# A mixture-of-experts layer's first product as seven block products instead of eight

## The chip, the core and the metric

The kernel runs on one core of one Trainium2 chip. The metric is the device time of one execution in microseconds; the median of three runs before the change is 1262.46 us. The profile is of one further execution. Engines carry their short names in the rows: PE is TensorE's matmuls, PEld its weight loads, DVE is VectorE, ACT ScalarE, POOL GpSimd, SP the engine that issues the transfers.

## The reference, cut to what matters

Three layers stand one behind the other: an attention over 32 packed queries, a dense layer pair (MoE1, 512 to 2048 to 512), and MoE2, four experts whose outputs are added with weights per token. All tensors are float32; there are 2304 tokens.

```python
def _moe_ref(x, w_in, w_out):                 # MoE1
    h = x @ w_in                              # 2304x512 @ 512x2048
    g = h * (1.0 / (1.0 + np.exp(-1.702 * h)))
    return (g @ w_out).astype(np.float32)

def _moe2_ref(x, domain_probs, w1, w2):       # MoE2
    E = w1.shape[0]                           # 4 experts, w1: 4x512x1024, w2: 4x1024x512
    p = domain_probs / (domain_probs.sum(-1, keepdims=True) + 1e-09)
    out = np.zeros((N, D), dtype=np.float32)
    for e in range(E):
        h = np.maximum(x @ w1[e], 0.0)        # first product
        out += p[:, e:e + 1] * (h @ w2[e])    # second product
    return out.astype(np.float32)
```

## The kernel before, in words

Every large product is computed in three parts: each operand is split into a high half (a cast, by ScalarE) and a low half (the operand less the high half, by VectorE or GpSimd), and three matmuls add high times high, low times high and high times low into one PSUM bank (`PARTS`). The helper `split` (L155 to L157) does both steps.

Up to some 240 us the attention runs, mixed with the first conversions and the begin of MoE1; its order is written out by a planner (`Order`) inside a manually scheduled block. Behind that block stands the rest of MoE1 and all of MoE2 as a list of steps `moe`, issued in the order of the list; the framework orders each engine's instructions from that and from what is ready.

MoE1 makes four passes `a` over its 2048 features, each over eight blocks `j` of 288 tokens. `l1_first` (matmuls on L523) makes the hidden features, `l2_first` (L568) sums 12 matmuls into a bank, and `l2_out` adds the bank to the accumulator `ACC[j]` (ScalarE copies in the first pass on L588, VectorE adds later on L590). In the last pass `put_y` splits each result into high and low halves, with GpSimd making the low half; this is `Y`, the moving operand of MoE2.

MoE2 takes the 32 chunks of 128 hidden features (4 experts x 8) in eight passes of four chunks. In each pass it walks five token blocks of 512, 512, 512, 256 and 512 tokens. `l1_second` streams the block's 512 or 256 tokens against 12 weight tiles (4 slices of the 512 inputs x 3 parts, L607); ScalarE takes the relu as the high half (L616) and VectorE makes the low half from the same bank (L617). One step later `l2_second` multiplies each 128 tokens of it by the 512 columns of w2 (L632), summing all four chunks of the pass in one bank per 128 tokens; then one VectorE instruction scales by the token's probability and adds to the output accumulator `ACC2` (L651; ScalarE in the first pass, L649). Each chunk's weights are loaded once (two transfers of 256 KB, L192 and L196) and split by ScalarE and VectorE. In the last pass SP sends out each 128 tokens (L655).

All large tiles come from one pool, `big`, with 37 buffers and the single tag `b`, through `slot`. PSUM is one pool of eight banks, `psum`. The conversion of MoE1's weights (`convert`) uses a small pool of its own, `cv`.

Of the kernel before, what the change touches and what calls it, by code (L numbers as in the profile page):

```python
# [97 lines left out]
def packed_attention_moe_kernel(  # L98
# [446 lines left out]
    def put_y(t, tok, n, src):  # L545

        done = 0
        while done < n:
# [12 lines left out]

    def l2_first(a, j, t):
# [21 lines left out]
    def l2_out(a, j, t, ps):
        dst = ACC[j][:, t, :]
        yield ("ACT" if a == 0 else "DVE"), 0.45, 0
        if a == 0:
            nc.scalar.copy(out=dst, in_=ps[:, :HS])  # L588
        else:
            nc.vector.tensor_add(out=dst, in0=ps[:, :HS], in1=dst)  # L590
# [1 line left out]
        if a == n_pass1 - 1:
            put_y(t, j * HS, HS, dst)


    n_pass2 = len(chunks2) // CPP
    per_e = w1.shape[2] // 128 // CPP
# [2 lines left out]
    def l1_second(a, j, c):  # L600
        n = blocks[j][1]
        w = W["x", a * CPP + c, 0]
        ps = psum("ps_g")
        m = 0
        for wp, xp in PARTS:
            for kk in range(KD):
                nc.tensor.matmul(  # L607
                    out=ps[:, :n],
                    lhsT=w[:, wp, kk * 128:(kk + 1) * 128],
                    rhs=Y[j, kk][:, xp, :],  # L610
                    start=(m == 0),
                    stop=(m == 3 * KD - 1),
                )
# [7 lines left out]
        hid[a, j, c, 2] = h

    def l2_second(a, j, c):
        b0, n = blocks[j]
        w = W["x", a * CPP + c, 1]
        h = hid.pop((a, j, c, 2))
        nt = n // 128
        if c == 0:
            accs[j] = [psum("ps_o") for _ in range(nt)]
        for t in range(nt):  # L630
            for m, (wp, hq) in enumerate(PARTS):
                nc.tensor.matmul(  # L632
                    out=accs[j][t],
                    lhsT=h[:, hq, t * 128:(t + 1) * 128],
                    rhs=w[:, wp, :],
                    start=(c == 0 and m == 0),
                    stop=(c == CPP - 1 and m == 2),
                )
# [209 lines left out]
```

## Time and profile before

| | |
|---|---|
| three runs, us | 1261.56, 1262.46, 1264.24 |
| profiled execution, us | 1263.64 |
| its span from first to last instruction, us | 1261.5 |
| TensorE busy / mean granted clock | 1205.0 us (96%) / 0.973 |
| VectorE, ScalarE, GpSimd busy | 538.9, 380.8, 116.4 us |
| read from HBM, written | 48.01 MB, 4.72 MB |

A busy time is the union of the engine's instructions. Overlapping instructions count once in it, so a mean duration times the count can be more than the busy time. Idle time of an engine is put down to what ended it.

### The profile page before, as it was taken

To read this page: it belongs to the slowest core of one execution; us is meant where nothing else is said; L and a number is where in the kernel's file an instruction comes from. 1 tells how busy PE (TensorE), PEld (TensorE's weight loads), DVE (VectorE), ACT (ScalarE), POOL (GpSimd) and SP (SyncE) were. 2 spreads that over 40 slices of the span, in tenths; PEclk is the share of its full clock that TensorE was granted. 3 is DMA by queue.
4 is the path that set the end of the run, shared out by engine and by line. 5 is a ranking of instruction groups with operands and counts; after the bars stand their busy time and mean duration, and the time that the engine had idled before them with its cause. 6 is when DMAs were issued, how large, how long until landed. Compare 5 with 4: busy or idle time off the path is not lost.

```text
span 1261.5 us, 16419 instructions
## 1 busy us (share of the span) xinstructions
PE 1205.0 (96%) x6816; PEld 1038.0 (82%) x6816; DVE 538.9 (43%) x961; ACT 380.8 (30%) x846; POOL 116.4 (9%) x142
## 2 busy tenths in 40 slices
PE   5769778999999999999999999999999999999998
PEld 4457578999999998888888888888888888888887
DVE  4873578787775541122233133233223224134222
ACT  3568654444444541222121121112112112012111
POOL 1320023221222330000000000000000000000000
PEclk8769889999999999999999999999999999999999
DMA  8822311121200110010010011001001002001011
GB/s 227 230 72 48 101 36 34 51 67 51 68 18 2 50 51 1 1 35 17 1 51 17 1 34 34 1 18 49 1 10 58 1 1 67 1 1 50 34 67 50
DMA packets 73482, 53.78 MB, mean 43 GB/s; under 512 B 43456, under 2 KB 62912, under 8 KB 73408
## 3 DMA queue, kind: packets, MB, share of 16 engines
q1 hardware_dynamic: 73408, 52.74, 14.1%
q8 instruction: 53, 0.87, 0.3%
q14 instruction: 21, 0.17, 0.0%
HBM read 48.01 MB, written 4.72 MB: 42 GB/s over the span
## 4 chain that ended last, share of the span: by engine, by line
PE 89%; DVE 4%; ACT 3%; issue 1%; DMA 1%; SPq 1%; POOL 1%; POOLq 0%; ACTq 0%; DVEq 0%
PE ps_g L607 31%; PE ps_o L632 31%; PE ps_acc L568 14%; PE ps_h L523 7%; PE ps_w L491 2%; PE ps_s L319 1%; PE ps_t L308 1%; SPq L279 1%; DMA raw<-in_moe_w_in_dram 1%; ACT L539 1%; DVE ex L250 0%; DVE man L246 0%; DVE pw L509 0%; ACT L374 0%; PE ps_v L399 0%
## 5 line engine op out<-in xcount | busy, mean ns | idle before, releaser
L632 PE MATMUL ps_o<-w,h 128*128 128x512 f32 x1728 | 421.7, 392 | 0.0
L607 PE MATMUL ps_g<-y,w 128*128 128x512 f32 (+1 forms) x1920 | 420.0, 368 | 0.0
L607 PEld LDWEIGHTS ps_g<-y,w 128*128 128x128 f32 x1920 | 338.6, 188 | 63.3
L632 PEld LDWEIGHTS ps_o<-w,h 128*128 128x128 f32 x1728 | 322.4, 188 | 68.0
L617 DVE SCALAR_TENSOR_TENSOR h<-ps_g,h 128x512 fp32r<-128x512 f32 (+1 forms) x160 | 102.0, 638 | 534.1 <-ACT h L616 534.1
L616 ACT ACTIVATE h<-ps_g 128x512 fp32r<-128x512 f32 (+1 forms) x160 | 88.7, 554 | 607.8 <-PE ps_g L607 607.8
L568 PE MATMUL ps_acc<-h,wout 128*128 128x288 f32 x1536 | 230.3, 298 | 2.1 <-DVE h L543 2.0
L568 PEld LDWEIGHTS ps_acc<-h,wout 128*128 128x128 f32 x1536 | 213.1, 190 | 5.7 <-DVE h L543 2.7
L523 PE MATMUL ps_h<-a,pw 128*128 128x288 f32 x768 | 129.0, 303 | 16.6 <-ACT a L468 13.7
L523 PEld LDWEIGHTS ps_h<-a,pw 128*128 128x128 f32 x768 | 112.6, 193 | 20.1 <-ACT a L468 14.5
L543 DVE TENSOR_TENSOR h<-g,h 128x288 fp32r<-128x288 f32 x128 | 68.6, 537 | 72.0 <-ACT g L540 70.9
L651 DVE SCALAR_TENSOR_TENSOR o<-ps_o,pr,o 128x512 f32<-128x512 f32 x126 | 86.1, 742 | 2.1 <-PE ps_o L632 2.1
L539 ACT ACTIVATE h<-ps_h 128x288 fp32r<-128x288 f32 x128 | 53.0, 414 | 79.3 <-PE ps_h L523 78.8
L157 DVE TENSOR_TENSOR w<-raw,w 128x512 fp32r<-128x512 f32 x64 | 44.2, 692 | 35.0 <-ACT w L156 31.8
L540 ACT ACTIVATE g<-ps_h 128x288 f32<-128x288 f32 x128 | 52.5, 410 | 0.2
L156 ACT CAST w<-raw 128x512 fp32r<-128x512 f32 x64 | 39.2, 620 | 41.6 <-DMA raw<-in_moe_w_dram 24.6
L590 DVE TENSOR_TENSOR acc<-ps_acc,acc 128x288 f32<-128x288 f32 x96 | 43.3, 451 | 10.8 <-PE ps_acc L568 9.9
L509 DVE TENSOR_TENSOR pw<-ps_w,pw 64x512 fp32r<-64x512 f32 x64 | 43.0, 687 | 7.2 <-ACT pw L505 6.0
L239 POOL TENSOR_SCALAR ex<-ex 128x512 uint32<-128x512 uint32 x32 | 29.4, 920 | 125.1 <-DVE ex L236 121.4
L505 ACT CAST pw<-ps_w 64x512 fp32r<-64x512 f32 x64 | 36.4, 579 | 10.7 <-PE ps_w L491 8.4
L157 POOL TENSOR_TENSOR y<-acc,y 128x288 fp32r<-128x288 f32 (+6 forms) x48 | 28.1, 599 | 52.5 <-ACT y L156 51.3
L246 DVE SCALAR_TENSOR_TENSOR man<-raw,man 128x512 f32<-128x512 uint32 x32 | 27.8, 868 | 0.4
(74 smaller groups left out, 551.3 us busy)
## 6 DMA issues: line engine op xcount, KB each, us to landing
raw<-in_moe_w_dram SPq DMA_DIRECT2D x64, 256.0 KB, 2.9
raw<-in_moe_w_in_dram SPq DMA_DIRECT2D x16, 512.0 KB, 3.8
raw<-in_moe_w_out_dram SPq DMA_DIRECT2D x16, 512.0 KB, 3.7
kv<-in_k_dram SPq DMA_DIRECT2D x32, 144.0 KB, 3.5
q<-in_q_dram SPq DMA_DIRECT2D x32, 144.0 KB, 2.8
out_dram<-o SPq DMA_DIRECT2D x18, 256.0 KB, 2.0
kv<-in_v_dram SPq DMA_DIRECT2D x16, 144.0 KB, 3.3
kv<-in_v_dram SPq DMA_DIRECT2D x8, 288.0 KB, 3.8
```

Source lines behind the costliest of these rows:

```text
L157: eng.tensor_sub(out=lo, in0=src, in1=hi.bitcast(F32))
L523: nc.tensor.matmul(out=ps[:, :HS], lhsT=PW[a, b, g][:, wp, c * 128:(c + 1) * 128], rhs=A[b * UG + g][:, xp, s * HS:(s + 1) * HS], start=(m ...
L539: nc.scalar.activation(out=h[:, 0, :], in_=ps[:, :HS], func=AF.Gelu_apprx_sigmoid)
L540: nc.scalar.activation(out=g32, in_=ps[:, :HS], func=AF.Gelu_apprx_sigmoid)
L543: nc.vector.tensor_sub(out=h[:, 1, :], in0=g32, in1=h[:, 0, :].bitcast(F32))
L568: nc.tensor.matmul(out=ps[:, :HS], lhsT=W["out", a, c][:, wp, t * 128:(t + 1) * 128], rhs=hid[a, j, c // 2][:, 2 * (c % 2) + hq, :], start ...
L590: nc.vector.tensor_add(out=dst, in0=ps[:, :HS], in1=dst)
L607: nc.tensor.matmul(out=ps[:, :n], lhsT=w[:, wp, kk * 128:(kk + 1) * 128], rhs=Y[j, kk][:, xp, :], start=(m == 0), stop=(m == 3 * KD - 1),)
L616: nc.scalar.activation(out=h[:, 0, :n], in_=ps[:, :n], func=AF.Relu)
L617: nc.vector.scalar_tensor_tensor(out=h[:, 1, :n], in0=ps[:, :n], scalar=0.0, in1=h[:, 0, :n].bitcast(F32), op0=ALU.max, op1=ALU.subtract,)
L632: nc.tensor.matmul(out=accs[j][t], lhsT=h[:, hq, t * 128:(t + 1) * 128], rhs=w[:, wp, :], start=(c == 0 and m == 0), stop=(c == CPP - 1 an ...
L651: nc.vector.scalar_tensor_tensor(out=acc, in0=ps[t], scalar=pr[:, tok, e:e + 1], in1=acc, op0=ALU.mult, op1=ALU.add,)
```

## The change

MoE2's first product, for two chunks (256 hidden features), two halves of the 512 inputs and two blocks of 384 tokens, is a product of a 2x2 block matrix of weights (A11 to A22) with a 2x2 block matrix of tokens (B11 to B22). It is now computed with the seven block products of Winograd's scheme instead of eight; each block product has 2 input slices x 3 parts = 6 matmuls of 384 columns. Sums of weight blocks (S1 to S4) and of token blocks (T1 to T4) are made ahead and split like the plain blocks; the four result blocks are sums of the seven products, made by VectorE in SBUF, from which relu and low half are then taken. MoE2 runs over three pairs of 768 tokens; within a pair over 16 "quads" of two chunks, so each weight is loaded, summed and split three times. The low halves of the weights are made by GpSimd. The second product sums over two chunks per bank, so each output tile is evicted 16 times in place of 8.

Around it: `big` has 29 buffers; the accumulators of MoE1 and of the output are three tiles of 768 tokens in a pool `yp` of their own, and `Y` is gone; `l2_out` writes in two pieces where a block crosses a pair's border; `convert` takes its scratch from `big` and `cv` is gone; `gp` has 6 buffers of 384 columns. The next pair's operands are made beside the last quad of a pair, the first pair's beside the last steps of MoE1.

```diff
+    TB = 384
+    NPAIR = NT // (2 * TB)
-    big = ctx.enter_context(tc.tile_pool(name="big", bufs=37))
+    big = ctx.enter_context(tc.tile_pool(name="big", bufs=29))
-    gp = ctx.enter_context(tc.tile_pool(name="gp", bufs=2))
-    cv = ctx.enter_context(tc.tile_pool(name="cv", bufs=2))
+    gp = ctx.enter_context(tc.tile_pool(name="gp", bufs=6))
+    yp = ctx.enter_context(tc.tile_pool(name="yp", bufs=NPAIR))
+    quads = [(i, e, c) for i in range(NPAIR) for e in range(NE) for c in range(w1.shape[2] // 256)]
-        man = cv.tile([128, 512], U32, tag="man", name="man")
-        ex = cv.tile([128, 512], U32, tag="ex", name="ex")
+        work = slot([128, 2, 512], U32, "cvt")
+        man, ex = work[:, 0, :], work[:, 1, :]
...
+    PRODUCTS = ("A11 B11", "S2 T2", "S3 T3", "S1 T1", "A12 B21", "A22 T4", "S4 B22")
+    TOK = [x.split()[1] for x in PRODUCTS]
+    def b_operand(i):
+        y = ACC[i]
+        B = {f"B{r + 1}{b + 1}": y[:, 2 * r:2 * r + 2, b * TB:(b + 1) * TB] for r in range(2) for b in range(2)}
...
+        for n, name in enumerate(TOK):
+            if name == "T2":
+                one = slot([128, 2, TB], F32, "t1")
+                two = slot([128, 2, TB], F32, "t2")
+                nc.vector.tensor_sub(out=one, in0=B["B12"], in1=B["B11"])
+                nc.vector.tensor_sub(out=two, in0=B["B22"], in1=one)
+                src = two
+            elif name == "T3":
+                three = slot([128, 2, TB], F32, "t3")
+                nc.gpsimd.tensor_sub(out=three, in0=B["B22"], in1=B["B12"])
...
+            elif name == "T4":
+                nc.gpsimd.tensor_sub(out=two, in0=B["B21"], in1=two)
...
+            for kk in range(2):
+                hi, lo = Bop[i, name, 0, kk], Bop[i, name, 1, kk]
+                nc.scalar.copy(out=hi, in_=src[:, kk, :])
+                (nc.vector, nc.gpsimd)[kk].tensor_sub(out=lo, in0=src[:, kk, :], in1=hi.bitcast(F32))
+            yield
+    def fetch_w1(n):
+        if n < len(quads):
+            i, e, c = quads[n]
+            raw = raws["w1", n] = slot([128, KD, 256], F32, "raw1")
+            nc.sync.dma_start(out=raw, in_=w1[e][:, c * 256:(c + 1) * 256].rearrange("(k p) f -> p k f", p=128))
...
+    def w1_operand(n):
...
+        nc.vector.tensor_add(out=s1, in0=Am["A21"], in1=Am["A22"])
+        nc.vector.tensor_sub(out=s2, in0=s1, in1=Am["A11"])
+        yield
+        nc.vector.tensor_sub(out=s3, in0=Am["A11"], in1=Am["A21"])
+        nc.vector.tensor_sub(out=s4, in0=Am["A12"], in1=s2)
+        yield
+        operand(("S2", "S3"), S[:, 0:2])
+        yield
+        yield
+        operand(("A11", "A12"), raw[:, :, :128].rearrange("p (o k) f -> p o k f", k=2))
+        yield
+        operand(("A22",), Am["A22"])
+        yield
+        operand(("S1", "S4"), S[:, 2:4])
+        yield
...
+    def hidden(n, c, b, src):
+        h = h2[n, b][:, c]
+        nc.scalar.activation(out=h[:, 0, :], in_=src, func=AF.Relu)
+        nc.vector.scalar_tensor_tensor(
+            out=h[:, 1, :], in0=src, scalar=0.0, in1=h[:, 0, :].bitcast(F32), op0=ALU.max, op1=ALU.subtract,
+        )
+    def quad(n):
+        for b in range(2):
+            h2[n, b] = hp.tile([128, 2, 2, TB], F32R, tag="h", name=f"h{b}")
+        ps = product(n, 0)
+        P = f32_tile("p1")
+        nc.scalar.copy(out=P, in_=ps)
+        yield
+        ps = product(n, 1)
+        U = f32_tile("u")
+        nc.vector.tensor_add(out=U, in0=ps, in1=P)
+        yield
+        ps = product(n, 2)
+        UV = f32_tile("uv")
+        nc.vector.tensor_add(out=UV, in0=ps, in1=U)
+        yield
+        ps = product(n, 3)
+        C22 = f32_tile("c22")
+        nc.vector.tensor_add(out=C22, in0=ps, in1=UV)
+        nc.vector.tensor_add(out=U, in0=ps, in1=U)
+        hidden(n, 1, 1, C22)
+        yield
+        for k, c, b, more in ((4, 0, 0, P), (5, 1, 0, UV), (6, 0, 1, U)):
+            ps = product(n, k)
+            nc.vector.tensor_add(out=more, in0=ps, in1=more)
+            hidden(n, c, b, more)
+            yield
...
+    for n in range(len(quads) + 1):
+        none = iter(())
+        now = quad(n) if n < len(quads) else none
+        fetch_w1(n + 1)
+        after = w1_operand(n + 1) if n + 1 < len(quads) else none
+        w2_now = w2_operand(n) if n < len(quads) else none
+        tiles = list(range(2 * TB // 128))
+        for k in range(8):
+            next(now, None)
+            if k > 0:
+                if n == 0:
+                    if pos["m"] < len(moe):
+                        moe_step()
+                elif tiles:
+                    l2_second(n - 1, tiles.pop(0))
+            next(after, None)
+            next(w2_now, None)
+            if k == 5:
+                fetch_w2(n + 1)
+            if n % per_pair == per_pair - 1 and n // per_pair + 1 < NPAIR:
+                next(b_parts[n // per_pair + 1], None)
```

`product(n, k)` issues the six matmuls of one block product into one bank; `operand` inside `w1_operand` takes a buffer of `big` and calls `split` with GpSimd; `w2_operand` does the same for the two chunks of w2; `l2_second(n, t)` now issues six matmuls for one 128-token tile and evicts them at once.

## Rows read from the trace of the kernel before

**Rows 1.** The page: busy us, share of span; tenths per slice; GB/s moved

```profile
PE 1205.0 (96%) x6816; PEld 1038.0 (82%) x6816; DVE 538.9 (43%) x961; ACT 380.8 (30%) x846; POOL 116.4 (9%) x142
...
PE   5769778999999999999999999999999999999998
...
PEclk8769889999999999999999999999999999999999
...
GB/s 227 230 72 48 101 36 34 51 67 51 68 18 2 50 51 1 1 35 17 1 51 17 1 34 34 1 18 49 1 10 58 1 1 67 1 1 50 34 67 50
```

**Rows 2.** Chain of waits, 455 us to the end: start us, us, what

```profile
by line: PE ps_g L607 48.9%; PE ps_o L632 48.8%; PE ps_acc L568 1.3%; DVE o L651 0.3%; PE ps_h L523 0.2%; issue 0.0%
...
467.36 5.44 PE ps_g L607 x24
```

**Rows 3.** Timeline of weight loads: start us, us, engine, line, count

```profile
391.88 1.65 PEld L568 LDWEIGHTS ps_acc<-h,wout 128*128 128x128 f32 x12
...
394.27 1.65 PEld L568 LDWEIGHTS ps_acc<-h,wout 128*128 128x128 f32 x12
...
534.00 1.62 PEld L607 LDWEIGHTS ps_g<-y,w 128*128 128x128 f32 x12
...
536.83 1.62 PEld L607 LDWEIGHTS ps_g<-y,w 128*128 128x128 f32 x12
...
563.00 2.68 PEld L607 LDWEIGHTS ps_g<-y,w 128*128 128x128 f32 x12
...
568.47 2.68 PEld L607 LDWEIGHTS ps_g<-y,w 128*128 128x128 f32 x12
```

**Rows 4.** Instructions of line L607: ns min/median/max, first and last start

```profile
L607 PEld LDWEIGHTS ps_g<-y,w x1920: 187/188/192, 467.1 to 1251.4; 128*128 128x128 f32 x192
```

**Rows 5.** Groups by form, 460 to 1250 us: count | busy us, mean ns

```profile
L617 DVE SCALAR_TENSOR_TENSOR h<-ps_g,h 128x512 fp32r<-128x512 f32 x127 | 87.8, 691 | 453.2 <-ACT h L616 453.2
L651 DVE SCALAR_TENSOR_TENSOR o<-ps_o,pr,o 128x512 f32<-128x512 f32 x122 | 83.3, 742 | 0.0
L616 ACT ACTIVATE h<-ps_g 128x512 fp32r<-128x512 f32 x127 | 75.8, 597 | 507.8 <-PE ps_g L607 507.8
L157 DVE TENSOR_TENSOR w<-raw,w 128x512 fp32r<-128x512 f32 x60 | 41.4, 693 | 33.6 <-ACT w L156 30.5 <-PE ps_o L632 2.8
L156 ACT CAST w<-raw 128x512 fp32r<-128x512 f32 x60 | 36.9, 620 | 41.6 <-DMA raw<-in_moe_w_dram 24.6 <-PE ps_o L632 16.6
L616 ACT ACTIVATE h<-ps_g 128x256 fp32r<-128x256 f32 x32 | 12.3, 384 | 95.1 <-PE ps_g L607 95.1
```

**Rows 6.** Instructions of L543 and L590: ns min/median/max

```profile
L543 DVE TENSOR_TENSOR h<-g,h x128: 415/458/1030, 79.4 to 460.3; 128x288 fp32r<-128x288 f32 x128
L590 DVE TENSOR_TENSOR acc<-ps_acc,acc x96: 439/456/460, 230.0 to 467.5; 128x288 f32<-128x288 f32 x96
```

**Rows 7.** Timeline of VectorE, 806 to 812 us

```profile
808.66 2.71 DVE L651 SCALAR_TENSOR_TENSOR o<-ps_o,pr,o 128x512 f32<-128x512 f32 x4
```

**Rows 8.** Groups by form, 250 to 440 us: count | busy us, mean ns

```profile
L543 DVE TENSOR_TENSOR h<-g,h 128x288 fp32r<-128x288 f32 x74 | 40.5, 547 | 38.5 <-ACT g L540 38.0
L259 POOL TENSOR_TENSOR wout<-man,wout 128x512 fp32r<-128x512 f32 x8 | 10.3, 1290 | 21.2 <-ACT wout L257 21.2
L157 POOL TENSOR_TENSOR y<-acc,y 128x224 fp32r<-128x224 f32 x4 | 2.7, 670 | 5.8 <-ACT y L156 5.8
```

**Rows 9.** Busy us: PE, PEld, DVE, ACT, POOL; granted clock, DMA share, GB/s

```profile
340.00:380.00 40.00, 40.00 (x295) 39.48 (x294) 31.26 (x63) 17.45 (x42) 9.43 (x8) 1.00 0.09 27
600.00:1000.00 400.00, 400.00 (x1848) 333.46 (x1847) 120.14 (x185) 64.31 (x113) 0.00 (x0) 1.00 0.07 22
```

**Rows 10.** DMA issues by line: count, size, median us to landing

```profile
raw<-in_moe_w_in_dram SPq DMA_DIRECT2D x16, 512.0 KB, 3.8
```

**Rows 11.** Waits of the transfer queue: us in total, times, longest

```profile
SPq L192 <- DVE w L157: 517.5, 24, 79.4
SPq L296 <- PE ps_e L390: 19.4, 4, 8.0
```

More of the change, by code (lines that the diff above doesn't have):

```diff
@@ L580, in l2_first @@
         if a == 0 and t == 0:
-            ACC[j] = slot([128, KD, HS], F32, f"acc{j}")
+            for i in {p[0] for p in pieces_of(j)}:
+                if i not in ACC:
+                    ACC[i] = yp.tile([128, KD, 2 * TB], F32, tag="y", name=f"y{i}")
         order.add(l2_out(a, j, t, ps), 1, clock())
     def l2_out(a, j, t, ps):
-        dst = ACC[j][:, t, :]
         yield ("ACT" if a == 0 else "DVE"), 0.45, 0
[L587 to L590, printed above, removed]
@@ L591, in l2_out @@
-        order.free += 1
[L592 to L597, printed above, removed]
-    ACC2 = {}
[L600 to L603, printed above, removed]
+        for i, o, at, n in pieces_of(j):
+            dst, src = ACC[i][:, t, o:o + n], ps[:, at:at + n]
+            if a == 0:
+                nc.scalar.copy(out=dst, in_=src)
+            else:
+                nc.vector.tensor_add(out=dst, in0=src, in1=dst)
@@ L604, in l1_second, with w2_operand, product @@
+    def w2_operand(n):
+        raw = raws.pop(("w2", n))
+        for c in range(2):
+            yield
+            w = W2[n, c] = slot([128, 2, 512], F32R, "w2")
+            split(w[:, 0, :], w[:, 1, :], raw[:, c, :], nc.gpsimd)
+            yield
+    def product(n, k):
+        i = quads[n][0]
+        a, b = PRODUCTS[k].split()
+        ps = psum("ps_p")[:, :TB]
         m = 0
         for wp, xp in PARTS:
-            for kk in range(KD):
+            for kk in range(2):
                 nc.tensor.matmul(
[L608 to L612, printed above, removed]
+                    out=ps, lhsT=Wop[n, a, wp, kk], rhs=Bop[i, b, xp, kk], start=(m == 0), stop=(m == 5),
@@ L631, in l2_second @@
+    def l2_second(n, t):
+        i, e, c0 = quads[n]
+        b, o = divmod(t * 128, TB)
+        h = h2[n, b]
+        ps = psum("ps_o")
+        for c in range(2):
             for m, (wp, hq) in enumerate(PARTS):
                 nc.tensor.matmul(
[L633 to L637, printed above, removed]
-                )
@@ L657, in setup @@
+        if n + 1 == len(quads) or quads[n + 1][0] != i:
+            nc.sync.dma_start(out=out[tok * 128:(tok + 1) * 128, :], in_=acc)
     def setup():
@@ L672, in packed_attention_moe_kernel @@
     NB1 = 2 * B
-    steps2 = [(a, j, c) for a in range(n_pass2) for j in range(len(blocks)) for c in range(CPP)]
     moe = [(packed_w, (0, 0), None)]
@@ L741, in moe_step @@
             make_w()
+        for part in beside.get(tag, ()):
+            next(part, None)
     def moe_lane():
@@ L815, in packed_attention_moe_kernel @@
     norm_probs()
-    while pos["m"] < len(moe):
-        moe_step()
+    b_parts = {i: b_operand(i) for i in range(NPAIR)}
+    last = n_pass1 - 1
+    fetch_w1(0)
+    fetch_w2(0)
+    first = w1_operand(0)
+    beside = {}
+    for j in (6, 7):
+        for c in range(CPP):
+            beside["first", last, j - 1, c] = (b_parts[0], first)
+    while pos["m"] < len(moe) - CPP:
+        moe_step()
+    per_pair = len(quads) // NPAIR
+    for n in range(len(quads) + 1):
[19 more added lines that the diff above has]
+                next(b_parts[n // per_pair + 1], None)
 _INS = ['q', 'k', 'v', 'p', 'moe_w_in', 'moe_w_out', 'moe2_domain_probs', 'moe2_w1', 'moe2_w2']
```

148 lines of the change are left out of this document (61 added, 87 removed).

## The prediction

> **What bounds the kernel now.** I read the page's busy line and its 40 slices first [rows 1]: TensorE is busy 96% of the span, and from the eighth slice it has a 9 in every slice but the last, at a granted clock of 9 tenths or more. From 600 to 1000 us VectorE is busy 120 of 400 us, ScalarE 64, GpSimd 0 [rows 9]. So MoE2, the stretch that the change rewrites, is bound by how many columns TensorE streams. The chain of waits from 455 us to the end says the same [rows 2]: 48.9% is MoE2's first product (L607), 48.8% its second (L632), and it begins at 467.36. Nothing of the weight conversion, the relu or the output scaling is on it; VectorE has 0.3%, at the tail.
>
> The price of one matmul comes from the distance between equal groups of weight loads in the timeline [rows 3]. Twelve matmuls of 512 columns for each product take 568.47 - 563.00 = 5.47 us, so 0.228 us each. Twelve of 256 columns with six of 512 take 536.83 - 534.00 = 2.83; less 6 x 0.228 that leaves 0.122 each. Eighteen of 288 columns take 394.27 - 391.88 = 2.39, so 0.133 each. Over columns / 2.4 GHz these are 14.6, 14.9 and 12.8 ns: a nearly fixed addition. A load is 188 ns long [rows 4], but with 288 columns matmuls already follow each other in 133 ns, so loads overlap and don't set the pace.
>
> **The change, part by part.**
> *First product.* Before: 1920 matmuls, of which 384 have 256 columns (32 chunks x 12) and 1536 have 512: 1536 x 0.228 + 384 x 0.122 = 349.9 + 46.7 = 396.6 us. After: 3 pairs x 16 quads x 7 products x 6 matmuls = 2016 with 384 columns. That size doesn't stand in the trace; between 0.133 + (96 / 2.4) = 0.173 and 0.228 - (128 / 2.4) = 0.175 I take 0.174: 350.8 us. That is 45.8 us less, on the path. The bounds by rows are 0.160 (no addition, 28 us more gained) and 0.188 (the length of one load, 28 us lost); the nearest row, 288 columns, excludes the second.
>
> *Second product.* Sums over two chunks in place of four: still 1728 matmuls of 512 columns, 394 us. Only its evictions double, from 144 to 48 x 6 = 288, and all but 18 go to VectorE.
>
> *Cover: VectorE.* A quad now gives TensorE 42 x 0.174 + 36 x 0.228 = 15.5 us. In that time VectorE has seven additions of a PSUM bank (128x384; L617 takes 691 ns at 512 columns [rows 5]; with the slope of the next pair, 1.05 ns a column, 557), four subtractions for the low half of h, now with both inputs in SBUF (693 ns at 512, median 458 at 288 [rows 5, 6], so 558), six evictions at 742 ns [rows 5] and four weight sums of 256 columns (about 425). That is 3.9 + 2.2 + 4.5 + 1.7 = 12.3 us. Independent neighbours overlap: four evictions are done in 2.71 us in place of 4 x 0.742 [rows 7], 0.08 less per neighbour, some 1.3 us a quad, so 11. Against that, after the additions of products 5 to 7 VectorE waits for ScalarE's relu (384 ns at 256 columns, 597 at 512 [rows 5], so 0.49, with handovers 0.55), 1.65 us: behind the waiting subtraction stand the next eviction and the weight sums. Result 12.7 of 15.5.
>
> *Cover: GpSimd and what the two share.* The low halves of the weights move from VectorE to GpSimd: per quad five subtractions of 512 columns at 1290 ns and one of 256 (670 at 224 [rows 8], 2.15 a column: 738), so 7.2 us, 46% of the quad; in MoE2 it was idle before [rows 9]. VectorE's subtraction L543, both inputs in SBUF, has median 458 but maximum 1030 ns, and its mean from 250 to 440 us is 547; L590, with one input in PSUM, stays between 439 and 460 [rows 6, 8]. So collisions cost 89 ns an instruction where GpSimd is 24% busy [rows 9]. At 46% that is 0.17 us, and for a quad's eight such instructions 1.4 us: VectorE comes to 14.1 of 15.5. It is covered, with 1.4 us to spare. In favour of that: from 340 to 380 us VectorE is 78% busy and TensorE 40.00 of 40.00 us [rows 9]. Bounds: 0, and the rival "VectorE" below.
>
> The Trainium skill bears on this, SBUF — State Buffer, "Who interferes with whom": a VectorE instruction with two SBUF inputs and a GpSimd instruction that reads SBUF exclude one another for the whole instruction. By that rule the trace agrees (1030 ns against 458), and the time would be that of the rival below, since this change puts both kinds into every quad.
>
> *ScalarE and DMA.* ScalarE: five passes of 0.49, five casts of 512 columns at 0.62 [rows 5], one of 256: 6.0 us of 15.5. Weights are read three times: two transfers of 512 KB per quad, 68 GB/s, where the page's slices show 230 [rows 1]; such a transfer lands in 3.8 us [rows 10] and is issued a quad ahead. SP's queue also holds the 18 output transfers, six behind each pair's last evictions; the fetch of the next w1 is issued ahead of them. I cost this at nothing; if a fetch is late, each microsecond comes once per quad, 48 in all.
>
> *The boundary of two pairs.* Twice (quads 16 and 32) the operands of the next pair are made beside a quad. VectorE gets two subtractions of 768 columns (0.96) and seven of 384: 5.8 us. GpSimd gets two of 768 (1.84 by the slope of [rows 8]) and seven of 384 (1.01): 10.8, with its 7.2 now 18.0 of 15.5. ScalarE gets fourteen casts of 384 columns (0.62 less 128 x 0.83 ns, the slope of its relu: 0.51), 7.2, with its 6.0 still 13.2 of 15.5. With GpSimd busy throughout, a collision costs about 89 / 0.24 = 370 ns, for 17 instructions 6.3 us. VectorE: 12.7 + 5.8 + 6.3 = 24.8, 9.3 over. The two quads beside it have 1.4 each to spare and eight PSUM banks hold about 3 slots of 2.4 us, so about half is absorbed: 4 us each, 8 in all. Bounds: 0, and full exclusion, GpSimd's 18.0 + VectorE's two-input time 9.8 - 15.5 = 12.3 each, 25 in all. For the first pair this lies beside MoE1's last two blocks, where GpSimd's subtractions for Y [rows 8] go. A gain is excluded: work is only added.
>
> *The pools.* `big` shrinks from 37 to 29, but the eight accumulators leave it; by the code at most some 29 tiles other than accumulators live at once (26 after the first loads, then the transposed keys). Loads of queries waited for a buffer before too, 8.0 us at the longest [rows 11]. I take 2 us; bounds 0 (the written order of this stage stays, so nothing is gained) and 20, the total of those waits. Splitting two of eight accumulator writes into two adds 32 short instructions where VectorE has room: nothing.
>
> *Tail.* Both end with an eviction of 0.74 us and a transfer; unchanged.
>
> *Sum.* The profiled execution took 1263.64 us (its span 1261.5 and 2.1 around it). 1263.6 - 45.8 + 8 + 2 = 1227.8. It stood 1.2 above the median of the three runs, so 1226.6: **1227 us**.
>
> **The rivals.**
> (a) *All hidden*: the boundary is absorbed whole and the pools cost nothing: 1263.6 - 45.8 - 1.2 = 1217. For it: weight work can run ahead in free buffers. Against it: GpSimd's 18.0 in 15.5.
> (b) *VectorE becomes the bound, slower.* Place: every quad, at the relu wait and at collisions with GpSimd. No overlap of neighbours (12.3), all four relu waits (2.2) and each of eight instructions held by 0.29 us, as for L543 with half its worst excess of 0.57 [rows 6] (2.3): 16.8. It decides from 15.5 on; above it each microsecond is 48. 1.3 x 48 = 62, with 8 for the boundaries: 1217 + 70 = 1287. For it: 14.1 of 15.5 is a thin cover. Against it: after a relu GpSimd's operation starts behind a cast of 0.62 us, when VectorE's subtraction is already running.
> (c) *Weights late.* 19 buffers are left beside the pair's ten, and a quad asks for nine; where an operand waits for the buffer of the quad before, ScalarE's queue holds the relus behind it. For it: SP's fetches of MoE2's weights waited 517.5 us for buffers before [rows 11]. Against it: then 37 were full, now about 14 of 19. At 0.6 us a quad, 29 + 10: 1256; from 0.95 us on it is a loss.
> (d) *Attention starved*: the upper end of the pools: 1227 - 2 + 20 = 1245. TensorE idles there already: 5 to 9 tenths busy in the first six slices, at a clock of 6 to 9 tenths [rows 1]. Against it: the count of live tiles above.
> That the change doesn't remove the columns is excluded by the count; that 384 columns run at a weight load's pace is excluded above.
>
> **How the numbers follow.** Forecast 53% (own range 1217 to 1240), (a) 10%, (b) 16%, (c) 16%, (d) 5%. About 0.2%, 2.5 us, is what a measurement tells from no change. Faster: 53 + 10 + 5 and half of (c): 76%. Same: a quarter of (c), 4%. Slower: (b) and the last quarter of (c): 20%. The range 1214 to 1272 leaves out (b) and the worst of (c), 18%.
>
> **What would show it.** Right: six weight loads of a product 1.04 us apart; TensorE 9 in every slice but those of two boundaries; VectorE near 85 to 90%. Wrong: TensorE waiting for VectorE's evictions in every quad (b), for weights or h (c), or a later begin of MoE2 than 467 us (d). The forecast falls if the additions and relus of one slot take VectorE more than the 2.41 us that TensorE needs for a product and an eviction's tile.

## The result, and the profile after

The changed kernel takes 1250.39 us (median of four runs, 1249.05 to 1253.02) where the kernel before takes 1262.11 on the same chip (1261.56 to 1264.24): a ratio of 0.9907, 95% interval 0.9886 to 0.9927. The forecast was 1227. The direction was right and the time lies in the range, but of the 35 us that were to be gained only 11.7 came. The profiled execution took 1249.63 us, its span 1247.4.

The page of the kernel after; the lines answer to those of [rows 1], with the transfers' totals between:

```profile
PE 1175.7 (94%) x6912; PEld 1062.0 (85%) x6912; DVE 899.5 (72%) x1652; ACT 523.6 (42%) x1152; POOL 483.0 (39%) x409
...
PE   5778788999999989999999989999999999999998
...
PEclk8779989999999989999999989999999899999999
...
HBM read 81.56 MB, written 4.72 MB: 69 GB/s over the span
```

TensorE lost its 9 in two slices where it had one before, those that begin at 437 us (the end of MoE1) and at 717 us (the first boundary between pairs); the granted clock dips in these and in the one that begins at 967 us (the second boundary). That 81.56 MB are read in place of 48.01 costs nothing in the rest of MoE2, where TensorE streams without a gap, as the windows of the kernel after show (start:end, length, then busy us and count of PE, PEld, DVE, ACT and POOL; granted clock, DMA share, GB/s). The first and the last lie in the steady part, the second is the quad beside which the next pair's operands are made, the third and fourth are the two long quads behind it:

```profile
500.00:600.00 100.00, 100.00 (x499) 90.10 (x498) 74.20 (x135) 36.38 (x73) 50.63 (x41) 1.00 0.23 69
699.00:714.60 15.60, 15.60 (x79) 14.10 (x78) 13.31 (x19) 8.23 (x19) 12.54 (x10) 1.00 0.13 35
714.60:735.90 21.30, 18.09 (x80) 15.40 (x79) 12.68 (x24) 7.96 (x16) 14.10 (x13) 0.92 0.35 102
735.90:756.50 20.60, 17.94 (x80) 15.26 (x79) 15.11 (x26) 9.25 (x17) 9.94 (x8) 0.92 0.44 150
800.00:900.00 100.00, 100.00 (x501) 90.25 (x500) 75.70 (x136) 35.47 (x70) 47.67 (x38) 1.00 0.21 64
```

In the steady part the matmuls have the forecast's size. This is the timeline of the weight loads of the kernel after, to be read as [rows 3]: six loads of an output tile (L732), six of a product (L680), and so on.

```profile
1049.04 1.28 PEld L732 LDWEIGHTS ps_o<-w,h 128*128 128x128 f32 x6
1050.36 1.12 PEld L680 LDWEIGHTS ps_p<-b,w 128*128 128x128 f32 x6
...
1061.22 1.30 PEld L732 LDWEIGHTS ps_o<-w,h 128*128 128x128 f32 x6
```

A product and a tile together take (1061.22 - 1049.04) / 5 = 2.436 us, and a quad is six of these and one more product of 1.04: 15.66 us. The distance between the first weight loads of one quad and the next is 15.66 us in 41 of the 46 full quads (1 to 46, counted from 0) and 15.59 in quad 1. The four others are quad 16 (21.24), 17 (20.63), 32 (22.11) and 33 (17.72), just behind those beside which the next pair's operands are made (15 and 31). The 46 take 19.0 us more than 46 times 15.66; below this sum is called **the boundary loss**. **The loss at MoE1's end** is told by the weight loads of MoE1's first product (L500 after, L523 before): from its load 672 to its load 736 there are 24.4 us before and 32.6 after, 8.2 more.

So the missing gain is in two places. Against the forecast's span (1261.5 - 45.8 + 8 + 2 = 1225.7) the span of 1247.4 is 21.7 longer: the 48 quads are 0.144 us longer each (15.66 in place of 42 x 0.174 + 36 x 0.228 = 15.516; 6.9), the boundaries cost 19.0 in place of 8 (11.0), MoE1's end costs 8.2 in place of 0, and the stages before it are 2.8 us early in place of 2 late (-4.8). That makes 21.3.

**What stands still at a boundary.** The timeline of the kernel after at the first one, only the instructions that carry the chain (idle time before an instruction and what ended it in brackets):

```profile
705.21 1.18 DVE L615 TENSOR_TENSOR b<-t,b 128x384 fp32r<-128x384 f32 x1
...
705.94 1.33 POOL L615 TENSOR_TENSOR b<-t,b 128x384 fp32r<-128x384 f32 x1
...
708.73 0.54 DVE L615 TENSOR_TENSOR b<-t,b 128x384 fp32r<-128x384 f32 x1
...
710.88 0.93 ACT L614 CAST b<-y 128x384 fp32r<-128x384 f32 x2 [1.82 <-POOL w L154]
...
711.42 0.82 DVE L615 TENSOR_TENSOR b<-y,b 128x384 fp32r<-128x384 f32 x1 [1.48 <-ACT b L614]
...
712.17 0.54 DVE L714 TENSOR_TENSOR c<-ps_p,uv 128x384 f32<-128x384 f32 x1
...
716.76 0.43 DVE L649 TENSOR_TENSOR s<-raw 128x256 f32<-128x256 f32 x1 [1.78 <-DMA raw<-in_moe_w_dram]
...
718.44 0.55 DVE L689 SCALAR_TENSOR_TENSOR h<-p,h 128x384 fp32r<-128x384 f32 x1
...
719.04 0.50 PE L732 MATMUL ps_o<-w,h 128*128 128x512 f32 x1 [1.47 <-DVE h L689]
...
728.29 0.42 DVE L649 TENSOR_TENSOR s<-raw 128x256 f32<-128x256 f32 x1 [0.95 <-DMA raw<-in_moe_w_dram]
...
729.47 0.62 ACT L153 CAST w<-s 128x512 fp32r<-128x512 f32 x1 [3.24 <-DVE s L650]
...
730.17 1.37 POOL L154 TENSOR_TENSOR w<-s,w 128x512 fp32r<-128x512 f32 x1 [2.56 <-ACT w L153]
...
734.78 0.62 ACT L153 CAST w<-s 128x512 fp32r<-128x512 f32 x1 [3.34 <-POOL w L154]
735.86 1.33 DVE L689 SCALAR_TENSOR_TENSOR h<-c,h 128x384 fp32r<-128x384 f32 x1 [3.42 <-ACT h L688]
...
742.09 1.39 PE L732 MATMUL ps_o<-w,h 128*128 128x512 f32 x3 [2.07 <-ACT h L688]
```

In these rows each engine takes its instructions in the order of its queue, and the work for the next quads stands there between the links of the chain that feeds TensorE now. There are two stalls.

**The first** (quad 16): TensorE waits 1.47 us for a low half of h (L689) that VectorE starts at 718.44. The 1.78 us that VectorE waits for a transfer just before (L649, the first weight sum) look like the cause, but the same wait stands in the steady part, where TensorE loses nothing. Three rows of the kernel after, from the quad that starts at 620.67:

```profile
629.14 0.55 DVE L714 TENSOR_TENSOR c<-ps_p,uv 128x384 f32<-128x384 f32 x1
...
633.91 1.29 DVE L649 TENSOR_TENSOR s<-raw 128x256 f32<-128x256 f32 x1 [1.95 <-DMA raw<-in_moe_w_dram]
...
635.46 0.54 DVE L689 SCALAR_TENSOR_TENSOR h<-p,h 128x384 fp32r<-128x384 f32 x1
```

There L714, the addition of the fourth product, starts 8.47 us after the quad and the low half (L689) 14.79. In quad 15, which starts at 698.97, it is 13.20 and 19.47: both 4.7 later. So VectorE is late before it comes to the transfer. Between stand the subtractions for the next pair's operands (L615): some are held while GpSimd works (1.18 us at 705.21, 0.54 at 708.73), and one waits 1.48 for ScalarE's cast, which has waited 1.82 for a buffer that GpSimd still reads.

**The second** (quad 17) does begin at a late transfer, by these rows. At 728.29 VectorE's weight sum has waited 0.95 for it; ScalarE's cast of the sums has waited 3.24 for VectorE, GpSimd's low half 2.56 for ScalarE. So GpSimd frees its buffer late: at 734.78 ScalarE has waited 3.34 us for it (L153 behind L154), the relu stands behind, VectorE's low half waits 3.42 for that, TensorE later 2.07.

No engine is full over the two quads: in the windows from 699.00 and 714.60 VectorE is 13.31 of 15.60 and 12.68 of 21.30 us busy, GpSimd 12.54 and 14.10, ScalarE 8.23 and 7.96.

The transfers are late because their own queue is in order too. This is the queue of transfers (SP) in the kernel after, from the steady part into the boundary, and then what it waited for between 660 and 760 us (total, times, longest):

```profile
660.53 0.37 SPq L622 DMA_DIRECT2D raw<-in_moe_w_dram  x1
...
676.26 0.37 SPq L622 DMA_DIRECT2D raw<-in_moe_w_dram  x1
...
703.38 0.37 SPq L628 DMA_DIRECT2D raw<-in_moe_w_dram  x1
713.42 0.37 SPq L622 DMA_DIRECT2D raw<-in_moe_w_dram  x1
```

```profile
SPq L628 <- PE ps_p L680: 26.7, 1, 26.7
...
SPq L622 <- POOL w L154: 15.1, 5, 9.6
```

The fetch of w1 (L622) comes every 15.7 us, but the one after 676.26 only at 713.42, 37.2 later: the fetch of w2 ahead of it (L628) waited 26.7 us for a buffer that the products (L680) still read, then L622 waited up to 9.6 for one that GpSimd read. The new pair's operands are taken from the same pool `big`, and the old pair's are read to the end of quad 15.

**The end of MoE1** has waits of both kinds. Timeline of the kernel after:

```profile
440.45 0.62 ACT L153 CAST w<-s 128x512 fp32r<-128x512 f32 x1 [4.14 <-POOL b L615]
...
440.98 0.41 ACT L516 ACTIVATE h<-ps_h 128x288 fp32r<-128x288 f32 x1
...
444.79 0.47 DVE L649 TENSOR_TENSOR s<-raw 128x256 f32<-128x256 f32 x1 [1.80 <-DMA raw<-in_moe_w_dram]
...
446.81 0.61 PE L528 MATMUL ps_acc<-h,wout 128*128 128x288 f32 x1 [3.46 <-DVE h L520]
```

ScalarE's cast for MoE2's weights waits 4.14 us for a buffer that GpSimd reads, and MoE1's own activation (L516) is behind it. Then VectorE's sum of quad 1's weights waits for a transfer issued 3.4 us before, and MoE1's low half of h (L520) is behind that; TensorE waits 3.46. These rows alone don't say which of the two sets the loss.

### The profile page after: what moved, and what is told of

It reads as the page before. It is cut to its first block, busy times and chain, and to the rows that moved or that the text cites. A ratio compares the mean times of both kernels' runs of the same rounds, so it can differ in the third digit from the quotient of the medians.

```text
span 1247.4 us, 18269 instructions
## 1 busy us (share of the span) xinstructions
PE 1175.7 (94%) x6912; PEld 1062.0 (85%) x6912; DVE 899.5 (72%) x1652; ACT 523.6 (42%) x1152; POOL 483.0 (39%) x409
## 3 DMA queue, kind: packets, MB, share of 16 engines
HBM read 81.56 MB, written 4.72 MB: 69 GB/s over the span
## 5 line engine op out<-in xcount | busy, mean ns | idle before, releaser
L732 PE MATMUL ps_o<-w,h 128*128 128x512 f32 x1728 | 449.9, 396 | 9.7 <-ACT h L688 5.5
L680 PE MATMUL ps_p<-b,w 128*128 128x384 f32 x2016 | 402.8, 339 | 0.6 <-DVE o L743 0.6
L680 PEld LDWEIGHTS ps_p<-b,w 128*128 128x128 f32 x2016 | 362.8, 189 | 24.6 <-DVE o L743 0.9
L732 PEld LDWEIGHTS ps_o<-w,h 128*128 128x128 f32 x1728 | 323.4, 189 | 63.6 <-DVE h L689 7.2
L154 POOL TENSOR_TENSOR w<-raw,w 128x512 fp32r<-128x512 f32 x192 | 236.4, 1250 | 172.3 <-ACT w L153 170.5
L743 DVE SCALAR_TENSOR_TENSOR o<-ps_o,pr,o 128x512 f32<-128x512 f32 x270 | 200.0, 741 | 5.1 <-PE ps_o L732 5.1
L154 POOL TENSOR_TENSOR w<-s,w 128x512 fp32r<-128x512 f32 x96 | 132.6, 1381 | 170.4 <-ACT w L153 170.4
L500 PE MATMUL ps_h<-a,pw 128*128 128x288 f32 x768 | 129.9, 305 | 19.1 <-ACT a L446 12.6
L153 ACT CAST w<-raw 128x512 fp32r<-128x512 f32 x192 | 106.9, 562 | 72.4 <-POOL w L154 48.0
L500 PEld LDWEIGHTS ps_h<-a,pw 128*128 128x128 f32 x768 | 113.6, 195 | 22.9 <-ACT a L446 13.4
L520 DVE TENSOR_TENSOR h<-g,h 128x288 fp32r<-128x288 f32 x128 | 73.4, 575 | 63.0 <-ACT g L517 62.0
L649 DVE TENSOR_TENSOR s<-raw 128x256 f32<-128x256 f32 x48 | 48.5, 1010 | 86.1 <-DMA raw<-in_moe_w_dram 69.8
L516 ACT ACTIVATE h<-ps_h 128x288 fp32r<-128x288 f32 x128 | 53.1, 415 | 96.5 <-PE ps_h L500 95.9
L706 DVE TENSOR_TENSOR u<-ps_p,p 128x384 f32<-128x384 f32 x48 | 26.7, 556 | 70.4 <-ACT p L702 67.2
L153 ACT CAST w<-s 128x512 fp32r<-128x512 f32 x96 | 59.1, 615 | 41.9 <-DVE s L650 19.2
L553 DVE TENSOR_TENSOR y<-ps_acc,y 128x288 f32<-128x288 f32 (+2 forms) x120 | 44.7, 388 | 11.2 <-PE ps_acc L528 11.0
```

The lines of the kernel that those rows point to most:

```text
L153: nc.scalar.copy(out=hi, in_=src)
L154: eng.tensor_sub(out=lo, in0=src, in1=hi.bitcast(F32))
L500: nc.tensor.matmul(out=ps[:, :HS], lhsT=PW[a, b, g][:, wp, c * 128:(c + 1) * 128], rhs=A[b * UG + g][:, xp, s * HS:(s + 1) * HS], start=(m ...
L516: nc.scalar.activation(out=h[:, 0, :], in_=ps[:, :HS], func=AF.Gelu_apprx_sigmoid)
L520: nc.vector.tensor_sub(out=h[:, 1, :], in0=g32, in1=h[:, 0, :].bitcast(F32))
L553: nc.vector.tensor_add(out=dst, in0=src, in1=dst)
```

## The experiments

All are edits of the changed kernel. Each ratio is to the kernel before, on the same chip, with its 95% interval. "Quads" are the long ones of the first boundary, with their us.

| run | median us | ratio | boundary loss | quads | loss at MoE1's end |
|---|---|---|---|---|---|
| the change | 1250.39 | 0.9907 [0.9886, 0.9927] | 19.0 | 16: 21.24, 17: 20.63 | 8.2 |
| e1_one_operand | 1241.57 | 0.9821 [0.9806, 0.9835] | 8.2 | 17: 19.68 | 8.2 |
| e2_no_operands | 1232.97 | 0.9754 [0.9738, 0.9770] | 0 | none | 8.1 |
| e3_big27 | 1248.95 | 0.9879 [0.9865, 0.9894] | 12.6 | 16: 22.01 | 3.1 |
| e4_w1_two_ahead | 1246.71 | 0.9863 [0.9845, 0.9881] | 10.8 | 16: 20.62, 17: 16.18 | 7.2 |
| e5_operands_vector | 1235.15 | 0.9768 [0.9745, 0.9790] | 9.2 | 18: 19.99 | 0.6 |
| e6_sums_gpsimd | 1249.34 | 0.9887 [0.9864, 0.9911] | 20.2 | 16: 19.45, 17: 21.92 | 4.9 |
| e7_both | 1235.42 | 0.9774 [0.9752, 0.9795] | 11.2 | 17: 20.14, 18: 17.40 | 0.0 |
| e8_first_pair_early | 1252.21 | 0.9905 [0.9886, 0.9924] | 18.6 | 16: 21.23, 17: 20.29 | 8.2 |
| e9_vector_w1_ahead | 1232.26 | 0.9752 [0.9734, 0.9770] | 0.4 | 17: 16.06 | 4.0 |
| e10_w2_vector | 1225.41 | 0.9699 [0.9683, 0.9715] | 0 | none | 0.6 |
| e11_vector_one_operand | 1234.42 | 0.9765 [0.9743, 0.9786] | 10.1 | 17: 17.85, 18: 19.59 | 0.6 |
| e12_w2_vector_alone | 1250.46 | 0.9895 [0.9877, 0.9913] | 17.2 | 16: 19.77, 17: 16.60, 18: 21.40 | 8.4 |

Losses and quads are those of the profiled execution. The stages before MoE1's last blocks are in no column: MoE1's load 576 starts between 378.7 and 388.8 us in these runs, in no order that the edits explain. A difference of a few us between two medians is therefore not read where the columns don't show it.

### Is it the operands, and is it their work or their buffers?

**e1_one_operand**

```diff
-  out=ps, lhsT=Wop[n, a, wp, kk], rhs=Bop[i, b, xp, kk], start=(m == 0), stop=(m == 5),
+  out=ps, lhsT=Wop[n, a, wp, kk], rhs=Bop[0, b, xp, kk], start=(m == 0), stop=(m == 5),
```

> The operands of pairs 1 and 2 are made as before (same instructions on VectorE, GpSimd and ScalarE, same order of steps), but the products of every pair read pair 0's operands, so the buffers of the new ones come free as soon as they are written; the output of pairs 1 and 2 is that of pair 0's tokens. Theory B (buffers: the next pair's ten operand buffers and three sums fill the 29, the fetch of the next w1 waits for a buffer, and VectorE's queue stands behind a weight sum that waits for that transfer): the four long quads (21.2, 20.6, 22.1 and 17.7 us) fall to about 15.7, some 19 us less, 1231. Theory E (engines: the additional 5.8 us of VectorE and 10.8 us of GpSimd with their collisions, as the prediction had it): they stay, 1250.

**e2_no_operands**

```diff
-  if n % per_pair == per_pair - 1 and n // per_pair + 1 < NPAIR:
-      next(b_parts[n // per_pair + 1], None)
...
-  rhs=Bop[i, b, xp, kk]
+  rhs=Bop[0, b, xp, kk]
```

> The operands of pairs 1 and 2 are not made at all; every pair reads pair 0's. No additional buffers and no additional work at the boundaries. Both theories: all quads 15.7 us, 1231; what e1 has above this is the price of the engines' work alone (B: under 3 us, E: 15 us or more).

Without the operands of the later pairs no quad is long, so the boundary loss comes from making them. When they are made and their buffers come free at once, the first stall is gone (quads 16 and 32 take 15.66) and the second stands as it was, in the timeline of e1_one_operand as in the change (2.07 us at 742.09):

```profile
736.79 1.57 PE L732 MATMUL ps_o<-w,h 128*128 128x512 f32 x3 [2.08 <-ACT h L688]
```

At the second boundary it is no smaller either (quad 33 takes 19.93, in the change 17.72). So held buffers have a part in the first stall, and no gain at the second shows. Neither edit touches MoE1's end.

**e3_big27**

```diff
-  big = ctx.enter_context(tc.tile_pool(name="big", bufs=29))
+  big = ctx.enter_context(tc.tile_pool(name="big", bufs=27))
```

> Only the pool big goes from 29 to 27 buffers. Theory B: the long quads grow, by some 2 to 10 us in sum, and so does the stop at the end of MoE1; steady quads keep 15.7 as long as some 14 of 17 are in use. 1254 to 1265. Theory E: same as the changed kernel, 1250.

A miss. Fewer buffers should have cost more; the second stall went, the loss at MoE1's end fell to 3.1, and what was won there was lost before it (load 576 came 10 us later). In this run the number of buffers didn't act as a size. That it moved the fetches and with them the order in the queues is likely, but not shown.

### The late transfer, and GpSimd's share of the operands

**e4_w1_two_ahead**

```diff
+  fetch_w1(1)
...
-  fetch_w1(n + 1)
+  fetch_w1(n + 2)
```

> The fetch of each quad's w1 is issued one quad earlier, so that at a boundary it takes its buffer ahead of the next pair's operands; one buffer more is held all the time. Theory B: VectorE's weight sums find their transfer landed; the long quads lose about half of their 19 us, 1238 to 1245, less if the missing buffer only moves the wait to the weight operands. Theory E: 1250.

**e5_operands_vector** (T3, T4 and all low halves of the token operands by VectorE)

```diff
-  nc.gpsimd.tensor_sub(out=three, in0=B["B22"], in1=B["B12"])
+  nc.vector.tensor_sub(out=three, in0=B["B22"], in1=B["B12"])
...
-  nc.gpsimd.tensor_sub(out=two, in0=B["B21"], in1=two)
+  nc.vector.tensor_sub(out=two, in0=B["B21"], in1=two)
...
-  (nc.vector, nc.gpsimd)[kk].tensor_sub(out=lo, in0=src[:, kk, :], in1=hi.bitcast(F32))
+  nc.vector.tensor_sub(out=lo, in0=src[:, kk, :], in1=hi.bitcast(F32))
```

> The token operands' sums T3, T4 and all their low halves are made by VectorE, none by GpSimd (seven subtractions of 384 and two of 768 columns move). Theory G (at a boundary GpSimd's backlog is what holds: ScalarE's casts wait for buffers that it still reads, the relus stand behind the casts): the 19 us of the four long quads fall to 8 or less, 1239. Theory V (VectorE's own load at the boundary is what holds): 3.9 + 1.9 us more of it, 19 grows to 25 or more, 1256.

**e9_vector_w1_ahead** (e5 with e4; the last line stands for its three)

```diff
+  fetch_w1(1)
...
-  fetch_w1(n + 1)
+  fetch_w1(n + 2)
...
+  nc.vector.tensor_sub(out=lo, in0=src[:, kk, :], in1=hi.bitcast(F32))
```

> e5 (all token operands by VectorE) with the fetch of w1 issued one quad earlier. If what is left at the boundaries (9.2 us in e5, a quad with 20 us in place of 15.7, where VectorE waits 1.4 us for a weight transfer and ScalarE's casts for GpSimd) comes from the late transfer, it falls to 2 or less, 1228; if it comes from GpSimd's burst of weight subtractions after the boundary, it stays, 1235.

These make a table of two by two for the boundary loss:

| | w1 fetched one quad ahead | two quads ahead |
|---|---|---|
| GpSimd makes its share | 19.0 | 10.8 |
| VectorE makes all | 9.2 | 0.4 |

Fetching w1 earlier is worth 8.2 in the first row and 8.8 in the second, GpSimd's share 9.8 and 10.4: two causes that add. The quads say which stall each takes: fetched earlier, the second is gone (quad 17 takes 16.18) and the first stays; with all on VectorE the first is gone and the second comes one quad later, in quad 18, with the same form in the timeline of e5_operands_vector (there too a weight sum has waited for its transfer before, 0.55 us at 732.85):

```profile
740.41 0.62 ACT L153 CAST w<-s 128x512 fp32r<-128x512 f32 x1 [2.68 <-POOL w L154]
...
741.49 1.33 DVE L689 SCALAR_TENSOR_TENSOR h<-c,h 128x384 fp32r<-128x384 f32 x1 [4.35 <-ACT h L688]
...
748.31 1.65 PE L732 MATMUL ps_o<-w,h 128*128 128x512 f32 x3 [2.67 <-ACT h L688]
```

That the first stall stays in e4 bears out the reading above. In the timeline of e4_w1_two_ahead VectorE's weight sum waits for nothing, and TensorE waits for the low half all the same:

```profile
722.77 0.53 DVE L649 TENSOR_TENSOR s<-raw 128x256 f32<-128x256 f32 x1
...
725.15 0.50 PE L732 MATMUL ps_o<-w,h 128*128 128x512 f32 x1 [0.90 <-DVE h L689]
```

L714 of quad 15 starts 14.49 us after the quad in e4 and 13.20 in the change, but 11.12 in e1, 10.09 in e5 and 9.80 in e9, where quad 16 takes 15.66. (In e6 and e12, where part of the first stall is left, it is 11.16 and 10.46; there more waits come behind it.) How much of VectorE's lateness is GpSimd holding its subtractions, and how much the casts that wait for GpSimd's buffers, no run separates.

e5 also took MoE1's end from 8.2 to 0.6. There fetching earlier did little (7.2 are left in e4, where the sum of quad 1's weights waits for nothing) and beside e5 even cost 3.4 (4.0 in e9). So GpSimd's share sets most of that loss too.

### Is it VectorE's load?

**e6_sums_gpsimd** (S1 to S4; the first and the last shown)

```diff
-  nc.vector.tensor_add(out=s1, in0=Am["A21"], in1=Am["A22"])
+  nc.gpsimd.tensor_add(out=s1, in0=Am["A21"], in1=Am["A22"])
...
-  nc.vector.tensor_sub(out=s4, in0=Am["A12"], in1=s2)
+  nc.gpsimd.tensor_sub(out=s4, in0=Am["A12"], in1=s2)
```

> The four weight sums S1 to S4 of every quad are made by GpSimd, so that no instruction of VectorE waits for a weight transfer. Theory Q (a sum that waits for its transfer stands ahead of relu's low halves in VectorE's queue): the stop at the end of MoE1 (8.2 us) falls to about 2 and the boundaries lose some 8 of 19 us, 1235. Theory G: GpSimd gets 3 us more in every quad, 21 us at a boundary quad of 15.7: the boundaries lose 25, 1256; the end of MoE1 stays.

**e7_both** (e5 with e6)

```diff
+  nc.gpsimd.tensor_add(out=s1, in0=Am["A21"], in1=Am["A22"])
...
+  nc.vector.tensor_sub(out=lo, in0=src[:, kk, :], in1=hi.bitcast(F32))
```

> e5 and e6 in one: GpSimd has the weights' sums and low halves (10.2 of 15.7 us in every quad, boundaries too), VectorE everything of the tokens. Theories G and Q together: end of MoE1 2, boundaries 5, 1230. Theory V: boundaries 22 or more, 1250.

e6 takes from VectorE both the wait for the transfer and work, and the boundary loss is 20.2: a miss for the view that the sums at the head of VectorE's queue are all there is. Beside e5 it changed nothing that the runs can tell (1235.42 against 1235.15).

**e10_w2_vector** (e5, and the low halves of w2 by VectorE)

```diff
-  split(w[:, 0, :], w[:, 1, :], raw[:, c, :], nc.gpsimd)
+  split(w[:, 0, :], w[:, 1, :], raw[:, c, :], nc.vector)
...
+  nc.vector.tensor_sub(out=lo, in0=src[:, kk, :], in1=hi.bitcast(F32))
```

> e5 with the low halves of w2 made by VectorE too: GpSimd has 4.6 us of 15.7 in every quad, VectorE 1.4 more (some 13). If GpSimd's burst after the boundary makes the rest, the 9.2 us fall to 3 or less, 1229. If VectorE's load counts now, steady quads grow above 15.7 or the boundaries above 9: 1240 and more.

No quad is long and MoE1's end costs 0.6: 1225.41 us, faster than both kernels. Windows of e10_w2_vector, the second over its first boundary, the third at MoE1's end:

```profile
500.00:600.00 100.00, 100.00 (x500) 90.14 (x499) 87.51 (x151) 36.76 (x70) 29.61 (x24) 1.00 0.23 73
700.00:800.00 100.00, 100.00 (x499) 90.12 (x498) 87.24 (x155) 44.25 (x89) 38.78 (x31) 1.00 0.32 101
430.00:450.00 20.00, 19.67 (x148) 19.44 (x147) 19.33 (x38) 14.05 (x36) 6.11 (x5) 1.00 0.09 28
```

The last stretch in the kernel after:

```profile
430.00:450.00 20.00, 15.05 (x99) 14.35 (x98) 15.92 (x22) 11.72 (x31) 18.24 (x15) 0.89 0.09 27
```

VectorE is 87.51 of 100 us busy and TensorE 100.00. At MoE1's end VectorE is 19.33 of 20 us busy and TensorE 19.67; in the kernel after VectorE has 15.92, GpSimd 18.24, and TensorE 15.05. VectorE's load did not set the loss.

### Two that missed, and one that moved nothing

**e11_vector_one_operand** (e5 with e1)

```diff
-  rhs=Bop[i, b, xp, kk]
+  rhs=Bop[0, b, xp, kk]
...
+  nc.vector.tensor_sub(out=lo, in0=src[:, kk, :], in1=hi.bitcast(F32))
```

> e5 with the products of every pair reading pair 0's operands (pairs 1 and 2 give pair 0's result): the operands are made, but their buffers come free at once. If the rest of 9.2 us is due to buffers held by two pairs at once, the boundaries fall below 1 us, 1226; if it is the engines' work, 9 stays, 1235.

**e12_w2_vector_alone** (the second edit of e10 without the first)

```diff
-  split(w[:, 0, :], w[:, 1, :], raw[:, c, :], nc.gpsimd)
+  split(w[:, 0, :], w[:, 1, :], raw[:, c, :], nc.vector)
```

> The changed kernel with only the low halves of w2 moved from GpSimd to VectorE (the token operands stay split between the two). By theory G GpSimd's load in a boundary quad falls from 18.0 to 15.4 us, about a quad's 15.7: the boundaries lose 3 to 8 in place of 19 us, the stop at the end of MoE1, where GpSimd has the first pair's operands and little of w2, stays at 5 to 8: 1235 to 1240. By theory V VectorE has 2.6 us more in every quad without losing any at the boundaries: 1255 or more.

Both are to be read by the quads. e1 and e5 each take the first stall away, so together they take no more, and the second is left in quads 17 and 18. In e12 most of the first is left at the first boundary (quad 16 takes 19.77) and less at the other (quad 32 takes 18.23). Quad 18 (21.40) is another stall; what sets it was not isolated.

**e8_first_pair_early**

```diff
-  for j in (6, 7):
+  for j in (5, 6):
```

> The first pair's operands and the first weights are made beside MoE1's last steps one block (9.6 us) earlier. If the work bunched there makes the stop of 8.2 us at the end of MoE1, it moves earlier and gets about half as long, 1246; if the sum of quad 1 that waits for its late transfer makes it (Q), it stays where it is, 1250. The boundaries stay at 19 in both.

The edit did not move the work: MoE2's first weight sum starts 43.19 us after load 576 here and 43.18 in the change, the first operand subtraction 41.54 and 41.52. So all losses are those of the change, and the run speaks for neither of its two answers. Whether an earlier place would have helped at MoE1's end is open.

Open as well: the two edits of e10 save 9.8 and 1.8 at the boundaries alone and 19.0 together, so the second is worth its price only when the first stall is gone. The order within the queues is set anew by each build, and no run held it fixed while one wait was changed.

## Why the prediction was right and wrong

**Right: the first product.** Matmuls of 384 columns follow each other in 0.174 us (median distance of L680's weight loads), as forecast. (Of its three additions per matmul the one for 256 columns comes to 15.2 ns, not 14.9; nothing hangs on it.) **Nearly right: the quad**, 15.66 in place of 15.5, since a product and a tile take 2.436 and not 6 x 0.174 + 6 x 0.228 = 2.41. Over 48 quads that is 6.9 us, and e10_w2_vector doesn't take it back.

**Right, with a size too large: VectorE's cover.** Of the 14.1 us a quad 12.4 were work and collisions (11 + 1.4), the rest the wait for the relu; 75.70 of 100 us busy are 11.9 of 15.66. Collisions with GpSimd are there. The groups of the kernel after (500 to 670 us, count, busy, mean ns):

```profile
L649 DVE TENSOR_TENSOR s<-raw 128x256 f32<-128x256 f32 x11 | 12.0, 1088 | 22.6 <-DMA raw<-in_moe_w_dram 19.6 <-issue 2.9
L689 DVE SCALAR_TENSOR_TENSOR h<-u,h 128x384 fp32r<-128x384 f32 x11 | 6.8, 619 | 0.6 <-ACT h L688 0.6
...
L689 DVE SCALAR_TENSOR_TENSOR h<-uv,h 128x384 fp32r<-128x384 f32 x11 | 6.0, 541 | 0.0
...
L650 DVE TENSOR_TENSOR s<-s,raw 128x256 f32<-128x256 f32 x11 | 4.5, 408 | 0.0
```

The first weight sum (L649) takes 1088 ns where the same form takes 408 (L650) undisturbed; the other instructions with two SBUF inputs lie within 0.1 us of their free duration. That is some 0.8 us a quad, not 1.4. The Trainium skill's rule (SBUF — State Buffer, "Who interferes with whom") that one of the two waits out the other's whole instruction agrees with L649 and with the operands' subtractions above: 1.18 us for the one at 705.21, begun while GpSimd was at work, and 0.54 at 708.73, where GpSimd's next one begins behind it and takes 1.35 in place of 1.02. That it makes VectorE the bound, rival (b), does not: e10_w2_vector refutes it.

**Wrong: the boundary of two pairs.** "VectorE: 12.7 + 5.8 + 6.3 = 24.8, 9.3 over", half of it absorbed, 8 in all: 19.0 were measured. The step sized the boundary by how full VectorE would be, and VectorE was 13.31 of 15.60 us busy beside the operands and 12.68 of 21.30 in the stalled quad. What stops TensorE is the order in the queues: work for the next quads at the head of VectorE's or ScalarE's queue waits, for a cast or a buffer that GpSimd holds up or for a late transfer, and the low half or the relu stands behind it. The first stall goes with GpSimd's share (e5) or the held buffers (e1), the second with the earlier fetch (e4); with both gone (e9) 0.4 is left. That e1 comes to 8.2, near the forecast's 8, is a coincidence: it is the second stall, of another cause than the one priced.

**Wrong: the first pair.** "For the first pair this lies beside MoE1's last two blocks" priced the operands at nothing; 8.2 were measured. GpSimd was busy 18.24 of 20 us there, VectorE 15.92 and ScalarE 11.72; a cast waited 4.14 for GpSimd and a weight sum 1.80 for its transfer, with MoE1's own instructions behind. e5_operands_vector, without GpSimd's share, takes 7.6 of it back, the earlier fetch of e4 only 1.0.

**The rivals.** (c), weights late, named the link that failed: an operand waits for a buffer, and "ScalarE's queue holds the relus behind it". It placed it in every quad; it stops TensorE at the boundaries only, where two pairs' operands are in the pool. (d) did not come: the stages before 380 us were 2.8 us early. (a), 1217, was 8.4 below the best variant, 6.9 of them the quad's length.

## What to carry to other kernels

Where engines work off their queues in order, ask of each prefetched instruction not whether its engine has time but what it may wait for and what stands behind it: here VectorE, 70% busy over two quads (25.99 of 36.90 us), stopped TensorE, and VectorE, 87% busy in e10_w2_vector, didn't. A wait that stands beside a stall is not yet its cause: look for the same row in an undisturbed stretch, then take the wait away. Where a term has two causes, take each away alone and both together, and read which stretch each one clears, not only the sum.

## What was not expected of the hardware

A stall costs more than its idle time, since the granted clock falls behind it. Windows of the kernel after, at the first boundary:

```profile
719.00:721.00 2.00, 1.11 (x3) 0.48 (x3) 2.00 (x4) 1.34 (x4) 2.00 (x2) 1.00 0.00 0
721.00:723.00 2.00, 1.11 (x4) 0.89 (x4) 1.43 (x3) 0.00 (x0) 2.00 (x2) 0.78 0.15 30
723.00:725.00 2.00, 2.00 (x8) 1.90 (x7) 0.11 (x1) 1.19 (x3) 1.27 (x3) 0.50 0.85 258
...
727.00:729.00 2.00, 2.00 (x12) 1.75 (x11) 1.04 (x4) 0.00 (x0) 0.61 (x1) 1.00 0.03 11
```

From 717 to 723 us TensorE is idle for 3.2 of 6 us; from 721 to 727 the granted clock is below full, down to half (1.2 of 2.4 GHz), and it is full again behind. Over quad 16 TensorE is busy 18.09 us for what takes 15.70 elsewhere: of the 5.6 us more (21.30 - 15.70) 3.2 are idle time and 2.4 longer matmuls. The mean granted clock of 0.92 makes 21.30 x 0.08 = 1.7 of these; the rest goes with matmuls that stand alone, such as the one at 719.04, 0.50 us long. In quad 17 it is 2.7 and 2.2, of which the clock makes 20.60 x 0.08 = 1.6. The prediction's boundary had no such term.
